# Early folds moved to GpSimd, free PSUM banks for the MLP, low value rows copied by DMA: one change to a fused attention, Fourier-mix and MLP kernel

## The chip, the cores and the metric

The kernel runs on one core of one Trainium2 chip. A core has TensorE (PE in the profile; PEld is its weight load), VectorE (DVE), ScalarE (ACT), GpSimd (POOL) and SyncE (SP, which here only issues transfers), and 16 DMA engines that all queues share. The metric is the device time of one execution in microseconds (us), as the median of several runs. For the kernel before, seven runs gave 291.88 to 294.54 us, with a median of 293.13 us.

## The reference, cut to what matters

Inputs are q, k, v of shape (4, 8, 768, 64) in float32, eight memory keys and values for each head, and two MLP weights of 512 x 2048 and 2048 x 512. Batch is 4.

```python
# attention, for chunks of 32 queries: 8 memory rows, 16 rows of left and 8 of right context
scores = scale * np.matmul(q_c, k_full.transpose(0, 1, 3, 2))
a = softmax(scores)                       # with 1e-09 added to the sum
out[:, :, c_start:c_end] = np.matmul(a, v_full)

# x: attention output as (4, 768, 512)
mixed = np.real(np.fft.fft(np.fft.fft(x, axis=1), axis=2))
u = x + mixed
un = (u - u.mean(-1)) / sqrt(u.var(-1) + 1e-06)
return u + np.maximum(un @ w_ch1, 0.0) @ w_ch2
```

So three things are computed for each batch, one after the other: chunked attention, the real part of a two-dimensional Fourier transform over rows and columns, and a normalised MLP with a residual.

## The kernel before, in words

**Attention.** The program goes through 16 pairs of heads, four for each batch; pair n is handled by `attention(n)`. q and k of a pair are loaded as bfloat16 from GpSimd's queue (`e_load_qk`, L324) into three rotating buffers each, and are turned by TensorE (`e_turn_q`, `e_turn_k`, L351) and copied out of PSUM (L360, L379). v of a pair is loaded by seven transfers from SP's queue (`e_load_v`, L333, L337, L342) into one of four buffers `va`. The partitions 0 to 31 of each `va` buffer hold no values and must be zero: ScalarE writes them once (`e_low_rows`, L312). GpSimd or VectorE write the ones and the zero edges (`e_edges`, `e_edge_ones`). For each pair there are two groups g, one for each half of the 768 rows: scores (L392), exponential on ScalarE (L400), values (L416), and a normalisation on VectorE (L426, L427) that writes `xsb`, the 768 x 512 rows of a batch, as six tiles of 128 rows.

**Fourier mix.** The transform is done with tables and uses its symmetries: sums and differences of rows and of columns, called folds, halve the work. For the first batch (`first_fourier`) the folds are done for each row half g as soon as its heads are there. `g_zy` (L556) adds or subtracts column halves of pairs 0 and 1, for parity `par` 0 and 1. `g_ff` with last = 0 (L569, L571, L574) folds the third pair in, and with last = 1 (L573, L574) the fourth. `g_hi` (L590) and `g_lo` (L594) split the result into two float16 parts, and TensorE multiplies with the row tables (`g_row` L614 with the mid column from `g_mid`, and `g_rows` L627). The sums in PSUM are taken out by L500 and L505, and the column tables follow (`e_columns`, L638). The later batches use `fourier(b)` (L488 for the rows), in which half of the rows is also sent through HBM to reverse their order.

**MLP.** VectorE adds the residual and takes the statistics (L644, L652, L653), ScalarE centres (L658), and the tile is turned: by TensorE for the first batch (L665, L676), by a DMA transpose from SP's queue for the others (`e_flip`, L670). `mlp(b)` then does, for two halves of 384 rows, 16 groups of the first product (`e_ch1`, L698, four matmuls a group, tile `ph`), a ReLU on ScalarE (L706), and three groups of the second product (`e_ch2`, L713, 16 matmuls a group, tile `pc`), whose result VectorE scales and adds to `xsb` (L720). The weights come by four transfers each from GpSimd's queue (L906 for the first, L910 for the second).

**PSUM banks.** Four banks serve as two pairs, `acc` and `mlp`. `mtag(b, i)` binds group i of the MLP to a pair: every third group to `acc`, the others to `mlp`. The same pairs hold `ps`, `pm`, `tp` and others.

**Order.** The order of the instructions on each engine is written out before the program is built. Each step is a task given to `Plan.add` with an engine, a cost, the tasks that it follows, the buffers that it takes and gives, and a rank. `Plan.order` walks through time with these costs and puts on each engine the task with the lowest rank that could start. SP's tasks stay in order unless they are loose; MLP groups have the highest ranks and fill what is left on TensorE. `Plan.share` models how transfers of several queues share the DMA engines. When TensorE would have nothing to do between the first scores and the first `lo`, the planner puts in a product of zeros (`e_fill`, L771, tile `idle`); these are fixed in the program. At run time each engine works off its own list in that order and waits on semaphores, so a late instruction holds up all that stand behind it on its engine. A change of one cost or rank can thus move instructions anywhere in the program.

In the profile's names, `in_q_dram` is q, `qs` and `ks` the loaded q and k, `trq` and `trk` their transposes in PSUM, `sc` scores, `e` the exponentials, `xa` and `xo` values in PSUM, `zy`, `ff`, `hi`, `lo` and `hl` the folds and their parts, `ps` rows, `up` and `dn` the taken-out rows, `pm` columns, `un` and `unT` the centred tile and its transpose, `w_sb` both MLP weights.

## Time and profile before

| what | value |
|---|---|
| median of 7 runs | 293.13 us (291.88 to 294.54) |
| the profiled execution's own time | 293.6 us |
| its span, first to last instruction | 291.9 us |
| TensorE busy | 274.7 us, 94% of the span |
| VectorE busy | 164.7 us, 56% |
| ScalarE busy | 164.9 us, 57% |
| GpSimd busy | 48.0 us, 16% |
| granted TensorE clock | 1.00 |
| moved by DMA | 38.36 MB, 131 GB/s over the span |

The page gives, for each engine, the time in which it was busy, a row of digits for 40 equal slices of the span (9 is 90% busy or more), the chain of work that ended last, and groups of like instructions. The time line lists instructions with start and length in us; an entry in brackets is how long the engine stood idle before it and what released it. A table by stretches gives the length of the stretch, then the busy time and the count of each engine, the granted clock, the mean share of the DMA engines and the GB/s. The profile is of one execution; times inside it are counted from the start of the span.

### The profile page before, as it was taken

The numbers are of one execution on the slowest core, as the hardware profiler recorded it, in microseconds if no ns is written. First come the engines' busy times: TensorE is split into PE (matmuls) and PEld (weight loads), VectorE is DVE, ScalarE is ACT, GpSimd is POOL, SyncE is SP. The second block draws the span as 40 slices with busy tenths as digits, with TensorE's granted clock in tenths as the row PEclk, the third lists the DMA queues.
The fourth block names the chain that finished last, engine by engine and source line by source line (L and its number), as shares of the span: only waits on it lengthen the run. The fifth ranks groups of instructions, "written<-read, shape, count | busy, mean of one in ns | idle before, by whom it ended". The sixth has DMA issues, their size and how long they took to land.

```text
span 291.9 us, 7349 instructions
## 1 busy us (share of the span) xinstructions
PE 274.7 (94%) x3055; PEld 173.3 (59%) x3055; DVE 164.7 (56%) x354; ACT 164.9 (57%) x294; POOL 48.0 (16%) x96
## 2 busy tenths in 40 slices
PE   1498998999999999999999999999899999999994
PEld 1376797765566767566777656656554644645641
DVE  7868998952249873948885878864912012012011
ACT  6796537687576586878885246432750721712700
POOL 8825641130222010121010021010020000000000
PEclk9999999999999999999999999999999999999999
DMA  6998999997999987698941357954221504004204
GB/s 102 204 186 139 211 209 195 197 198 150 176 222 272 146 228 105 92 155 218 185 80 61 37 130 196 145 145 108 56 54 72 110 0 122 25 36 108 38 36 108
DMA packets 98689, 38.36 MB, mean 131 GB/s; under 512 B 85728, under 2 KB 93920, under 8 KB 98656
## 3 DMA queue, kind: packets, MB, share of 16 engines
q1 hardware_dynamic: 87344, 21.83, 40.2%
q0 software_dynamic: 10592, 15.21, 28.3%
q10 hardware_dynamic: 720, 0.85, 0.9%
q8 instruction: 24, 0.39, 0.6%
q14 instruction: 9, 0.07, 0.1%
HBM read 37.36 MB, written 13.37 MB: 174 GB/s over the span
## 4 chain that ended last, share of the span: by engine, by line
PE 88%; DVE 4%; DMA 3%; ACT 1%; POOL 1%; issue 1%; POOLq 0%; DVEq 0%
PE pc L713 29%; PE ph L698 28%; PE xa L416 8%; PE ps L488 5%; PE sc L392 3%; PE pm L638 3%; DMA ks<-in_k_dram 3%; PE trk L351 2%; PE idle L771 2%; PE ps L627 2%; PE trq L351 2%; DVE st L652 1%; DVE xsb L644 1%; PE xo L416 1%; PE ps L614 1%
## 5 line engine op out<-in xcount | busy, mean ns | idle before, releaser
L706 ACT ACTIVATE hT<-ph 128x384 f16<-128x384 f32 x128 | 60.8, 492 | 52.9 <-PE ph L698 52.0
L698 PE MATMUL ph<-unT,w_sb 128*128 128x384 f16 x512 | 88.9, 326 | 0.9 <-ACT hT L706 0.6
L713 PE MATMUL pc<-w_sb,hT 128*128 128x512 f16 x384 | 88.0, 380 | 0.0
L698 PEld LDWEIGHTS <-w_sb 128*128 128x128 f16 x512 | 48.4, 98 | 33.2 <-issue 1.8
L713 PEld LDWEIGHTS <-hT 128*128 128x128 f16 x384 | 35.9, 98 | 40.6 <-issue 0.4
L720 DVE SCALAR_TENSOR_TENSOR osb<-pc,rstd,xsb 128x512 f32<-128x512 f32 x24 | 18.0, 749 | 72.4 <-PE pc L713 69.7
L400 ACT ACTIVATE e<-sc,mbias 128x384 f32<-128x384 f32 x64 | 33.6, 578 | 12.5 <-PE sc L392 12.0
L416 PE MATMUL xa<-va,e 128*64 128x65 f32 x672 | 26.5, 229 | 1.2 <-issue 1.2
L416 PEld LDWEIGHTS xa<-va,e 128*64 128x64 f32 x672 | 22.5, 141 | 8.2 <-issue 6.6
L658 ACT ACTIVATE un<-xsb,mu_s 128x512 f16<-128x512 f32 x24 | 17.2, 721 | 14.2 <-DVE mu_s L653 14.2
L500 ACT CAST up<-ps 128x386 f16<-128x386 f32 x16 | 9.7, 605 | 16.9 <-PE ps L488 15.6
L652 DVE BATCH_NORM_STATS2 st<-xsb 128x6 f32<-128x512 f32 x24 | 16.6, 690 | 0.7
L324 POOL DMA_DIRECT2D qs<-in_q_dram x16 | 10.5, 658 | 36.6 <-PE trq L351 21.9
L360 ACT COPY qT<-trq 128x768 bf16<-128x768 bf16 x16 | 12.7, 796 | 6.1 <-PE trq L351 6.1
L427 DVE TENSOR_TENSOR xsb<-xa,zs 128x384 f32<-128x384 f32 x28 | 15.6, 557 | 1.0
L505 DVE TENSOR_TENSOR up<-ps,up 128x386 f16<-128x386 f32 x16 | 9.5, 594 | 10.7 <-ACT up L500 10.7
L426 DVE RECIPROCAL zs<-xa 128x6 f32<-128x6 f32 x28 | 5.3, 190 | 17.4 <-PE xa L416 17.0
L351 PE MATMUL trq<-ident_b,qs 96*64 96x96 bf16 x256 | 9.1, 218 | 5.6 <-DMA qs<-in_q_dram 5.6
L324 POOL DMA_DIRECT2D ks<-in_k_dram x16 | 10.2, 638 | 22.6 <-PE trk L351 18.9
L379 ACT COPY kTb<-trk 128x1056 bf16<-128x1056 bf16 x12 | 12.5, 1040 | 2.2 <-PE trk L351 2.2
L644 DVE TENSOR_TENSOR xsb<-pm,xsb 128x512 f32<-128x512 f32 x15 | 10.1, 670 | 5.2 <-PE pm L638 5.2
L478 DVE TENSOR_TENSOR lo<-ff,hi 128x768 f16<-128x768 f32 x12 | 11.4, 954 | 2.5 <-ACT hi L473 2.2
(142 smaller groups left out, 327.3 us busy)
## 6 DMA issues: line engine op xcount, KB each, us to landing
va<-in_v_dram SPq DMA_DIRECT2D x32, 220.0 KB
w_sb<-in_moe_w_ch_dram POOLq DMA_DIRECT2D x8, 512.0 KB, 15.3
qs<-in_q_dram POOLq DMA_DIRECT2D x16, 192.0 KB, 6.2
ks<-in_k_dram POOLq DMA_DIRECT2D x16, 192.0 KB, 6.0
out_dram<-osb SPq DMA_DIRECT2D x12, 256.0 KB
x_rows<-xsb POOLq DMA_DIRECT2D x3, 768.0 KB, 5.1
xr<-x_back POOLq DMA_DIRECT2D x3, 768.0 KB, 5.5
out_rows<-osb SPq DMA_DIRECT2D x9, 256.0 KB
```

The costliest lines, as they stand in the source:

```text
L324: nc.gpsimd.dma_start(dst[n % NS][0:QP], src[b, 2 * pr:2 * pr + 2].rearrange("h (p j) d -> p h (j d)", j=RB))
L351: nc.tensor.transpose(out_[64 * hh:64 * hh + 64, j * w:(j + 1) * w], src[:, hh, j * D:(j + 1) * D], eye)
L400: nc.scalar.activation(e1[:, :, :, ts(half, 32)], sc[:, :, 0:6, ts(half, 32)], AFT.Exp, bias=mbias[:, half:half + 1], scale=1.0 / math.sqr ...
L416: nc.tensor.matmul(xa[64 * half:64 * half + 64, st, hh, 0:65], e1[:, hh, t6, :], v1[:, hh, 6 * g + t6, 0:65], start=True, stop=True)
L427: nc.vector.tensor_tensor(xs[b][:, 3 * g:3 * g + 3, 2 * pr * D:(2 * pr + 2) * D] .rearrange("p s (h d) -> p s h d", h=2), xa[:, :, :, 0:D] ...
L488: nc.tensor.matmul(out_[:, sp, :], part[:, ab, sp * 3 + st, c0:c1], tab[:, sp, st, :], start=(st == 0 and i == 0), stop=(st == 2 and i == 1))
L652: nc.vector.bn_stats(st6, xs[b][:, kt, :])
L658: nc.scalar.activation(un, xs[b][:, kt, :], AFT.Identity, bias=mu_of[b][:, kt, 0:1], scale=-1.0)
L698: nc.tensor.matmul(ph[:, 0:384], w1_sb[:, dt, ts(ht, P)], unT_of[b][:, dt, sh * 384:(sh + 1) * 384], start=(dt == 0), stop=(dt == NDT - 1))
L706: nc.scalar.activation(hT_of[b, sh][:, ht, :], ph[:, 0:384], AFT.Relu, bias=0.0, scale=-1.0)
L713: nc.tensor.matmul(pc_of[b, sh, stl], hT_of[b, sh][:, ht, ts(stl, P)], w2_sb[:, ht, :], start=(ht == 0), stop=(ht == NHT - 1))
L720: nc.vector.scalar_tensor_tensor(osb, pc, rstd_of[b][:, st:st + 1], xs[b][:, st, :], ALU.mult, ALU.add)
```

## The change

Three things are changed in what is computed where, and the planner's model is changed beside them.

1. The early folds of the first batch's second row half (`g_zy` with g = 1, and `g_ff` with g = 1 and last = 0) run on GpSimd and no longer on VectorE. Their tasks get ranks 20.1 to 20.3.
2. An MLP group no longer has a fixed pair of banks. `pick` names both pairs, and `Plan.order` takes the one whose bank has been free longest.
3. The low rows of `va[2]` and `va[3]` are filled by transfers from `va[0]` and `va[1]` on SP's queue, and no longer by ScalarE.

In the planner, the weight with which a transfer shares the DMA engines is now given for each task (`grain`) where it was fixed by queue, some costs of transfers are changed, and a DMA transpose holds SP for its cost. A path in which q and k are turned by DMA transposes is added for batches from `TURNED` = 9 on; there are four batches, so it isn't taken, but its two buffers `kU` are zeroed by GpSimd (`t_uz`).

```diff
     def e_low_rows(i):
         low = va[i][0:MEM0].rearrange("p h t c -> p (h t c)")
+        if i > 1:
+            nc.sync.dma_start(low, va[i - 2][0:MEM0].rearrange("p h t c -> p (h t c)"))
+            return
         nc.scalar.copy(low, zero[0:MEM0].to_broadcast([MEM0, 2 * NT * 66]))
...
-        xb, sl = xs[0], slice(3 * g, 3 * g + 3)
-        nc.vector.tensor_tensor(zy_of[0, par][:, sl], xb[:, sl, 0:P], xb[:, sl, HD:HD + P],
+        xb, sl, eng = xs[0], slice(3 * g, 3 * g + 3), nc.gpsimd if g == 1 else nc.vector
+        eng.tensor_tensor(zy_of[0, par][:, sl], xb[:, sl, 0:P], xb[:, sl, HD:HD + P],
                                 ALU.add if par == 0 else ALU.subtract)
...
+        eng = nc.gpsimd if g == 1 and not last else nc.vector
...
-        nc.vector.tensor_tensor(ff[:, :, 1:P], (ff if last else zy)[:, :, 1:P],
+        eng.tensor_tensor(ff[:, :, 1:P], (ff if last else zy)[:, :, 1:P],
                                 rev_ap(xb, 2 * P - 1 + HD * last, P - 1, [[DM, 3]]),
                                 ALU.add if plus else ALU.subtract)
...
-    def mtag(b, i):
-        return "acc" if i % 3 == 2 else "mlp"
+    pick_of = {}
+
+    def pick(*key):
+        return pick_of.setdefault(key, dict(of=("mlp", "acc")))
...
-        ph_of[b, sh, ht] = ph = bank(mtag(b, ht), [P, 512], FP32, "ph")
+        ph_of[b, sh, ht] = ph = bank(pick(b, sh, ht)["tag"], [P, 512], FP32, "ph")
...
-            pc_of[b, sh, stl] = bank(mtag(b, stl), [P, DM], FP32, "pc")
+            pc_of[b, sh, stl] = bank(pick(b, sh, stl, 0)["tag"], [P, DM], FP32, "pc")
...
-        t_low[i] = add("ACT", 1.45, lambda i=i: e_low_rows(i), [t_zero, e_],
-                       rank=(0, 1, 2, 3)[i])
+        t_low[i] = (add("ACT", 1.45, lambda i=i: e_low_rows(i), [t_zero, e_], rank=i) if i < 2 else
+                    add("SP", 0.5, lambda i=i: e_low_rows(i), [t_low[i - 2], e_], moved=0.7,
+                        grain=0.3, loose=True))
...
+    t_uz = add("POOL", 0.4, lambda: [nc.gpsimd.memset(kU[i], 0.0) for i in range(NKU)], rank=20)
...
-    for i in range(2, NV):
-        t_low[i]["behind"] = t_exp[i - 2, 1]
-        t_low[i]["rank"] = t_exp[i - 2, 1]["rank"] + 0.1
...
-                zy = add("DVE", 0.5, lambda par=par, g=g: g_zy(par, g),
+                early = ("DVE", "POOL")[g]
+                zy = add(early, 0.5 + 0.5 * g, lambda par=par, g=g: g_zy(par, g),
                          [t_norm[0, g], t_norm[1, g], t_sines],
-                         take=("unT",) if g == 0 else ())
+                         take=("unT",) if g == 0 else (), rank=20.1 if g else None)
                 for ab in range(2):
-                    pre[par, ab, g] = add("DVE", 0.62 if ab == 0 else 0.5,
+                    pre[par, ab, g] = add(early, (0.62 if ab == 0 else 0.5) + 0.5 * g,
                                           lambda par=par, ab=ab, g=g: g_ff(par, ab, g, 0),
-                                          [zy, t_norm[2, g]],
+                                          [zy, t_norm[2, g]], rank=20.2 + 0.1 * par if g else None,
```

In the planner, the choice of a bank and the new weight of a transfer read:

```diff
+                    take = t["take"]
+                    if t["pick"] is not None:
+                        take += tuple(sorted((x for x in t["pick"]["of"] if self.free[x] > 0),
+                                             key=lambda x: (since.get(x, []) + [0.0])[0]
+                                             + t["pick"]["of"].index(x) * 0.5))[:1] or ("",)
...
-            heads = [xs_[0] + [2.0 if q == "POOL" else 1.0] for q, xs_ in left.items() if xs_]
+            heads = [xs_[0] + [xs_[0][0]["grain"]] for q, xs_ in left.items() if xs_]
...
-                t_un[kt] = add("SP", 0.1, lambda kt=kt: e_flip(b, kt),
-                               [un, t_un.get(kts[i - 1]) if i else None],
-                               take=("unT",) if i == 0 else (), give=("un",), moved=0.8,
+                t_un[kt] = add("SP", 1.2, lambda kt=kt: e_flip(b, kt),
+                               [un], behind=t_un.get(kts[i - 1]) if i else None,
+                               take=("unT",) if i == 0 else (), give=("un",), late=1.6,
                                loose=True)
```

## The prediction

> **What bounds the kernel now.** I read four views: the page's slices and chain, the engines' busy time by stretches that I chose after reading the chain, the time line around 17 to 47 us, and TensorE's waits.
>
> ```profile
> PE 274.7 (94%) x3055; PEld 173.3 (59%) x3055; DVE 164.7 (56%) x354; ACT 164.9 (57%) x294; POOL 48.0 (16%) x96
> ...
> PE   1498998999999999999999999999899999999994
> ...
> PE 88%; DVE 4%; DMA 3%; ACT 1%; POOL 1%; issue 1%; POOLq 0%; DVEq 0%
> ```
>
> TensorE carries 88% of the chain. So the question is only where TensorE stands still, or runs the zero matmuls of L771 ("idle") that produce nothing. Busy time by stretches (length, TensorE, its weight loads, VectorE, ScalarE, GpSimd, clock, DMA), and then the idle matmuls alone in the same stretches:
>
> ```profile
> 0.00:17.00 17.00, 7.22 (x100) 4.56 (x102) 14.43 (x48) 12.28 (x17) 14.03 (x43) 1.00 0.98 155
> 17.00:34.20 17.20, 15.95 (x370) 12.07 (x369) 13.25 (x33) 12.22 (x20) 6.37 (x14) 1.00 1.03 176
> 34.20:47.30 13.10, 12.25 (x178) 11.10 (x178) 12.53 (x34) 7.95 (x16) 6.37 (x11) 1.00 1.10 206
> 47.30:56.70 9.40, 9.16 (x156) 7.80 (x153) 8.40 (x19) 5.40 (x10) 1.44 (x3) 1.00 1.22 198
> 56.70:201.00 144.30, 144.30 (x1794) 92.18 (x1793) 98.02 (x190) 93.04 (x167) 18.22 (x26) 1.00 0.83 155
> 201.00:210.00 9.00, 8.11 (x59) 5.29 (x57) 6.96 (x16) 4.90 (x11) 0.00 (x0) 1.00 0.29 71
> 210.00:287.70 77.70, 77.69 (x415) 40.33 (x413) 10.36 (x17) 29.16 (x60) 1.60 (x2) 1.00 0.26 64
> ...
> 17.00:34.20 17.20, 4.95 (x24) 1.00 1.03 176
> ```
>
> From 56.7 us (the first MLP matmul) to 287.7 TensorE loses 0.9 us in all. What a reordering can win after 17 us is therefore bounded: 17 to 34.2 us holds 1.25 idle and 4.95 of idle matmuls, 34.2 to 47.3 holds 0.85, 47.3 to 56.7 holds 0.24, 201 to 210 holds 0.89: 8.2 us together. In 34.2 to 47.3 VectorE is busy 12.53 of 13.10 us beside a TensorE that is busy 12.25: two engines close to full.
>
> **The trace around the edited steps** (start, length, engine, line, tiles):
>
> ```profile
> 17.85 1.50 ACT L312 COPY va<-zero 32x1584 f32<-32x1584 f32 x1
> 21.80 1.49 ACT L312 COPY va<-zero 32x1584 f32<-32x1584 f32 x1
> ...
> 31.84 0.55 DVE L574 TENSOR_TENSOR ff<-ff,xsb 128x381 f32<-128x381 f32 x1
> 31.95 0.50 POOL L600 TENSOR_TENSOR mid<-xsb 128x3 f32<-128x3 f32 x1 [1.85 <-DVE xsb L427]
> 32.79 0.20 POOL L603 TENSOR_TENSOR mid<-mid,mid 128x3 f16<-128x3 f32 x1
> ...
> 36.74 1.02 DVE L574 TENSOR_TENSOR ff<-zy,xsb 128x381 f32<-128x381 f32 x2
> 37.68 0.55 DVE L556 TENSOR_TENSOR zy<-xsb 128x384 f32<-128x384 f32 x1
> 38.34 1.01 DVE L574 TENSOR_TENSOR ff<-zy,xsb 128x381 f32<-128x381 f32 x2
> ```
>
> The last three lines are the early folds of the second row half: VectorE starts them at 36.67 and is through at 39.27.
>
> **What the Trainium skill says.** (1) "GPSIMD Engine Reference", section 3.1 Elementwise: a two-input tensor_tensor costs GpSimd about 2.6 cycles per element at 1.2 GHz. For 384 elements I estimate 0.83 us, say 0.9 with its start; no run here shows one yet, and VectorE needs 0.5 to 0.55. (2) "SBUF — State Buffer", section Who interferes with whom: a VectorE instruction with two SBUF inputs and a GpSimd instruction that reads SBUF exclude each other; the later one waits for the whole of the other. The trace agrees on GpSimd's side: three elements took 0.50 us at 31.95, ending as VectorE's fold ended (32.39), and a like operation 0.20 at 32.79 beside none. (3) "DMA: Bandwidth & Descriptors", section Issuing engines are not separate DMA queues: transfers from all engines share 16 DMA engines; the trace's DMA share is 0.98 to 1.22 up to 56.7 us, so what is added there delays something.
>
> **The change, part by part.** The planner writes out another order for every engine, so I compared the two built programs' instruction orders.
>
> *Folds.* VectorE loses the 2.60 us block (36.67 to 39.27) and one zy (0.5): 3.1 us. GpSimd gains six two-input folds, 6 x 0.9 = 5.4 us, three small ops, and two memsets of the otherwise unused kU buffers (128x1024 bf16; the nearest row, 4x1024 bf16, took 1.0 each: 2.0 us). The folds of each parity stand between normalisations of pairs 1 to 3 and VectorE's own folds, nearly all of them with two SBUF inputs. Bounds for what this costs VectorE: 0 if they interleave, 5.4 if each GpSimd fold holds VectorE throughout. I take half, 2.7: VectorE comes out 0.4 us ahead instead of 3.1.
>
> TensorE then takes all first-half rows (48 matmuls), mid rows and second-half rows without the transposes that stood between. The 96 rows and 24 mid-row matmuls cost 4 x 1.0 + 4 x 1.0 + 2 x 1.1 = 10.3 us; starting where they start now (34.2) they can't end before 44.5, and end now at 45.3. So even VectorE's full gain would be worth only 0.8 us here. I put 0.5 for TensorE waiting on the lo folds, then 0.95 (evacuation 0.6 at L500 and subtraction 0.6 at L505, less one transpose) before the columns, against 0.85 and 0.24 now: +0.4.
>
> *Low rows.* Removes the two ScalarE copies (1.5 each) at 17.85 and 21.80. The first holds an exponential up (19.25 rather than about 18.75), but the next thing in line is TensorE's gap of 1.24 us at 21.41 in the middle of a value product, released by nothing shown, with a 16 KB instruction packet moving from 20.1 to 21.3: I take it to recur at the same place in the program and to swallow the half microsecond. Two copies of 203 KB enter SP's queue before the third pair's values, which SP now issues from 12.72: about 1.6 us later. They are next needed at 26.3 and 30.1 (L416), and GpSimd's gate on the fourth pair's values moves from 24.93 to some 26.5, behind its zy folds anyway. Cost 0 while those 3 us of cover last, up to 1 without.
>
> *Third pair's ks.* Its transpose now stands ahead of the second score group, at 16.4, when TensorE is still slow (16 transposes 0.88 at 13.09, 0.35 at 19.26): +0.5. It lands at 16.0 now (issue 8.64 plus 7.4), so the bounds are +0.5 and +1.0. The fourth pair's q and k are issued behind the kU memsets, at 17.2 and not 15.2; they land at about 21.4 and 22.8 to 23.4, inside the same gap: 0 to 0.5. Idle matmuls: 24 become 25 after 17 us, with 7 to 4 near 25 us: +0.2 in count, -0.2 since the gap ends the same wait. Sum of these: +0.2 to +0.5; I take +0.2.
>
> *Queue of GpSimd.* The fifth pair's q and k stand where they stood, but the sixth pair's and the four weight loads w1 (L906) now wait for the last folds, so w1 goes from 27.93 to about 38.5: the mid operations end at 34.86, the last parity's folds take 2.0 and up to 0.7 of waiting, the q and k issues 1.3. Now the last chunk lands at 44.1, 16.2 after the first issue, with four q/k loads ahead of it that land some 1.4 apart; with two ahead I expect 52 to 54. The first MLP matmul, which needs all four, comes at about 55.7: covered by some 2 us. w2 and later q/k move with it and are needed later (72 and 79).
>
> *Banks.* `mtag` bound MLP group i to a bank pair; now the planner picks. The one place where TensorE waits for that is 207.7 to 209.6 (waits 0.31 and 0.58): -0.9.
>
> *Order.* Leaving a run of wide matmuls for scores, values or transposes costs 0.1 us each (four pc matmuls 0.97 before a transpose, 0.86 before another wide run). I count 48 such places against 44: +0.4. In the new order the second batch's first MLP group follows its third column group after 6.3 us, not 14.6; its transposed input takes 12.3 us from the first column matmul now (113.7 to 126), 0.85 less without an osb between, just in time at 129: +0.3.
>
> Sum: +0.4 +0.2 -0.9 +0.4 +0.3 = +0.4 us. On the profiled execution: span 291.9 to 292.3, its time 293.6 to 294.0. It lies 0.5 above the median of the runs (293.13), so the median becomes 293.5.
>
> **Rivals.**
> - *Held* (slower). GpSimd's folds hold VectorE for the full 5.4 us: VectorE is 2.3 us worse off, not 0.4 better, a difference of 2.7, of which TensorE passes on 2.2 once its 0.5 is used: 295.7. It decides once a fold takes over 0.9 us and VectorE's neighbours are the lo folds at L594. For: VectorE 96% busy there. Against: several of its operations there read PSUM (L426, L427, L379).
> - *Weights late* (slower). Each microsecond that w1's last landing exceeds 55.7 stops TensorE's queue for one. At 58 it costs 2.3: 295.8. For: DMA share over 1. Against: no weights compete with the value loads before 38 us any more.
> - *Front wins* (faster). The gap at 21.4 doesn't recur (-1.2), VectorE keeps its 3.1 us so the rows run unbroken (-0.5), and the early transpose is not slow (-0.5): 291.3. For: the ScalarE copies were real waits; against: the limit of 44.5 above.
> - *Banks do nothing*: the 0.9 at 208 returns under another name: 294.4, within the same class.
>
> **From cases to numbers.** No change within 0.5% (1.5 us) is what this kernel's measurements can't tell apart. Forecast with the bank variant: 0.45, its own range 292.1 to 294.9, split 0.04 faster, 0.36 same, 0.05 slower. Held 0.18 (0.14 slower, 0.04 same). Weights late 0.14 (0.12 slower, 0.02 same). Front wins 0.23 (0.20 faster, 0.03 same). Sums: faster 0.24, same 0.45, slower 0.31. The range 290.8 to 296.4 reaches into both sides; the unknown fold price and the landing of w1 set its upper end.
>
> **What would show it.** Right: first L698 matmul at 55 to 57 us; TensorE at 100% from there; no wait at 208; L556 and L574 on GpSimd near 0.9 us each, VectorE's L574 and L594 above 0.55 beside them. Wrong: a TensorE wait on w_sb at the first L698; new waits at L416 on va, at L351 on ks near 16.5, or at L698 on unT near 129; a first L698 before 54.5, which would mean the front wins.

## The result and the profile after

The changed kernel takes 295.65 us in the median (294.98 to 297.11) against 293.13 us (291.88 to 295.45): a ratio of 1.0085, 95% interval [1.0064, 1.0106], so 1.9 to 3.1 us slower. The likeliest case of the prediction, 293.5 and no change that can be told, did not come; the time lies in the predicted range. The profiled execution took 295.08 us (span 293.3) against 293.6 (291.9), only 1.5 us more. The ratios here and below leave out executions more than 1.5% above the fastest of their kernel (one of after_again, four of pick_alone, two of the kernel before); the medians keep them.

From the page of the changed kernel, engines and slices of TensorE, then the shares of the chain that ended last:

```profile
PE 276.0 (94%) x3056; PEld 173.1 (59%) x3056; DVE 164.0 (56%) x345; ACT 163.6 (56%) x292; POOL 58.4 (20%) x107
...
PE   1669999999999999979999999999999999999994
...
PE 79%; DMA 10%; POOL 7%; DVE 1%; issue 1%; ACT 1%; POOLq 0%; ACTq 0%
```

TensorE's share of the chain fell from 88% to 79%. DMA now has 10% and GpSimd 7%: the chain runs through the load of the third pair's ks, GpSimd's folds, the w1 loads and a transposing DMA of the second batch. The 7 in TensorE's row, at about 131 us, is new. Busy time in four of the stretches that the prediction used (length, TensorE, weight loads, VectorE, ScalarE, GpSimd, clock, DMA share, GB/s):

```profile
17.00:34.20 17.20, 15.98 (x362) 12.57 (x363) 12.98 (x32) 9.35 (x17) 8.11 (x13) 1.00 0.94 165
...
47.30:56.70 9.40, 8.97 (x152) 6.89 (x150) 8.90 (x21) 6.61 (x10) 2.13 (x3) 1.00 1.07 204
56.70:201.00 144.30, 142.79 (x1811) 89.98 (x1811) 94.28 (x186) 92.76 (x165) 20.51 (x29) 1.00 0.83 158
201.00:210.00 9.00, 9.00 (x74) 6.75 (x73) 4.04 (x7) 5.27 (x11) 0.00 (x0) 1.00 0.30 80
```

The last two rows answer the prediction at once. The 0.89 us at 208 are gone (9.00 of 9.00), and 1.51 us are lost between 56.7 and 201, where the kernel before lost nothing. The idle time in the first two, 1.22 and 0.43, is much as before (1.25 and 0.24). TensorE's waits (what it waited for: us in total, times, longest; the largest, 5.5 us for q at the start, was 5.6 before):

```profile
PE trk L375 <- DMA ks<-in_k_dram: 4.4, 3, 2.7
PE ph L741 <- DMA unT<-un: 1.5, 1, 1.5
...
PE ph L741 <- DMA w_sb<-in_moe_w_ch_dram: 0.4, 1, 0.4
```

TensorE's time line at these places (start, length, engine, line, tiles; in brackets the idle time before and what ended it), first at the third pair's ks, then at the first MLP group, then at the first one of the second batch:

```profile
17.82 0.88 PE L375 MATMUL trk<-turn_b,ks 100*64 100x100 bf16 x16 [2.66 <-DMA ks<-in_k_dram]
...
19.06 1.57 PE L456 MATMUL xa<-va,e 128*64 128x65 f32 x24
...
55.51 0.66 PE L741 MATMUL ph<-unT,w_sb 128*128 128x384 f16 x3
56.60 0.34 PE L741 MATMUL ph<-unT,w_sb 128*128 128x384 f16 x1 [0.43 <-DMA w_sb<-in_moe_w_ch_dram]
...
131.67 0.81 PE L741 MATMUL ph<-unT,w_sb 128*128 128x384 f16 x4 [1.51 <-DMA unT<-un]
```

The first ph starts at 55.51 (55.7 predicted, 56.69 before) and stops within its four matmuls for the last w1 chunk. And GpSimd's time line with the folds and the loads behind them:

```profile
27.05 2.13 POOL L596 TENSOR_TENSOR zy<-xsb 128x384 f32<-128x384 f32 x2 [8.87 <-DVE xsb L467]
...
31.38 1.31 POOL L615 TENSOR_TENSOR ff<-zy,xsb 128x381 f32<-128x381 f32 x1
...
36.20 0.40 POOL L644 TENSOR_TENSOR mid<-mid,mid 128x3 f16<-128x3 f32 x1
...
37.01 2.57 POOL L615 TENSOR_TENSOR ff<-zy,xsb 128x381 f32<-128x381 f32 x2
...
40.83 2.19 POOL L957 DMA_DIRECT2D w_sb<-in_moe_w_ch_dram  x4
```

The six folds (one of 1.28 at 32.69 isn't shown) take 7.3 us, not 5.4; w1 is issued from 40.83, not 38.5. The mid operations, which stand behind four of the folds in this queue, end at 36.60, where they ended at 34.86 before.

**Where the profiled time went.** TensorE's last matmul ends at 289.50 instead of 287.72, 1.8 later, and what follows is 0.4 shorter (3.8 against 4.2).

| term | from | us |
|---|---|---|
| front | first ph 1.18 earlier, but 24 value (0.85), 12 score (0.28) and 16 transposing matmuls (0.46) that stood ahead of it now stand behind | +0.4 |
| wait on w_sb | waits | +0.4 |
| wait on unT | waits | +1.5 |
| bank waits at 208 | stretches | -0.9 |
| more changes of tile shape on TensorE | 102 against 96 after 56.6 us, by 0.1 | +0.6 |
| sum, to compare with 1.8 | | +2.0 |

### The profile page after: what moved, and what is told of

Its sections match the earlier page's. It is cut to its first block, busy times and chain, and to the rows that moved or that the text cites. A ratio compares the mean times of both kernels' runs of the same rounds, so it can differ in the third digit from the quotient of the medians.

```text
span 293.3 us, 7347 instructions
## 1 busy us (share of the span) xinstructions
PE 276.0 (94%) x3056; PEld 173.1 (59%) x3056; DVE 164.0 (56%) x345; ACT 163.6 (56%) x292; POOL 58.4 (20%) x107
## 4 chain that ended last, share of the span: by engine, by line
PE 79%; DMA 10%; POOL 7%; DVE 1%; issue 1%; ACT 1%; POOLq 0%; ACTq 0%
PE ph L741 29%; PE pc L756 27%; PE xa L456 7%; PE ps L528 5%; DMA w_sb<-in_moe_w_ch_dram 5%; DMA ks<-in_k_dram 3%; PE pm L679 3%; PE sc L433 2%; PE trq L375 2%; PE trk L375 2%; DMA unT<-un 2%; POOL ff L615 1%; POOL qs L348 1%; PE pm L579 1%; POOL ks L348 1%
## 5 line engine op out<-in xcount | busy, mean ns | idle before, releaser
L749 ACT ACTIVATE hT<-ph 128x384 f16<-128x384 f32 x128 | 62.3, 491 | 56.0 <-PE ph L741 55.0
L741 PE MATMUL ph<-unT,w_sb 128*128 128x384 f16 x512 | 90.7, 327 | 1.9 <-DMA unT<-un 1.5
L741 PEld LDWEIGHTS <-w_sb 128*128 128x128 f16 x512 | 47.4, 98 | 33.6 <-issue 2.5
L699 ACT ACTIVATE un<-xsb,mu_s 128x512 f16<-128x512 f32 x24 | 17.2, 720 | 6.1 <-DVE mu_s L694 6.1
L375 PE MATMUL trk<-turn_b,ks 100*64 100x100 bf16 x256 | 9.7, 224 | 4.9 <-DMA ks<-in_k_dram 4.4
L348 POOL DMA_DIRECT2D ks<-in_k_dram x16 | 10.3, 642 | 17.0 <-PE trk L375 13.9
```

Of the source, the lines that this page charges most:

```text
L348: nc.gpsimd.dma_start(dst[n % NS][0:QP], src[b, 2 * pr:2 * pr + 2].rearrange("h (p j) d -> p h (j d)", j=RB))
L375: nc.tensor.transpose(out_[64 * hh:64 * hh + 64, j * w:(j + 1) * w], src[:, hh, j * D:(j + 1) * D], eye)
L699: nc.scalar.activation(un, xs[b][:, kt, :], AFT.Identity, bias=mu_of[b][:, kt, 0:1], scale=-1.0)
L741: nc.tensor.matmul(ph[:, 0:384], w1_sb[:, dt, ts(ht, P)], unT_of[b][:, dt, sh * 384:(sh + 1) * 384], start=(dt == 0), stop=(dt == NDT - 1))
L749: nc.scalar.activation(hT_of[b, sh][:, ht, :], ph[:, 0:384], AFT.Relu, bias=0.0, scale=-1.0)
```

## The experiments

Each run edits the changed kernel, unless it says otherwise, and leaves its planner alone: the order is the changed kernel's with the named tasks moved in the list that the planner returns (`behind(t, other)` puts t right after other in that list, which orders each engine's queue). Lines below the edit shift by a few. Ratios are to the kernel before, measured beside each run; "difference" is that ratio times 293.13.

| run | median | ratio, 95% | difference, us |
|---|---|---|---|
| the changed kernel | 295.65 | 1.0085 [1.0064, 1.0106] | +1.9 to +3.1 |
| after_again | 295.80 | 1.0078 [1.0046, 1.0110] | +1.3 to +3.2 |
| k15_late | 294.48 | 1.0049 [1.0027, 1.0071] | +0.8 to +2.1 |
| w1_late | 299.30 | 1.0203 [1.0144, 1.0263] | +4.2 to +7.7 |
| trk_back | 296.41 | 1.0112 [1.0079, 1.0145] | +2.3 to +4.3 |
| clear_trk | 297.10 | 1.0131 [1.0091, 1.0170] | +2.7 to +5.0 |
| no_clear | 296.24 | 1.0115 [1.0081, 1.0148] | +2.4 to +4.3 |
| folds_vector | 296.01 | 1.0114 [1.0079, 1.0150] | +2.3 to +4.4 |
| clear_trk_folds | 297.40 | 1.0150 [1.0121, 1.0179] | +3.5 to +5.2 |
| low_scalar | 294.18 | 1.0046 [1.0031, 1.0061] | +0.9 to +1.8 |
| pick_alone (on the kernel before) | 294.27 | 1.0012 [0.9986, 1.0038] | -0.4 to +1.1 |
| three_moves | 293.29 | 0.9997 [0.9974, 1.0020] | -0.8 to +0.6 |
| moves_split | 293.16 | 1.0006 [0.9988, 1.0024] | -0.4 to +0.7 |

**The granted clock.** The table by stretches also shows the clock that TensorE was granted. In some executions it stood at one half for 3.4 us, as here in trk_back:

```profile
25.20:28.60 3.40, 3.40 (x52) 2.22 (x44) 2.42 (x4) 1.05 (x2) 0.71 (x1) 0.50 0.62 131
```

One such stretch brings the mean over an execution to 0.994 or less, and that mean is on record for each execution. Of the 136 executions of the kernel before that were measured beside these runs and enter the ratios, 20 were that low; their median is 294.66 us, against 292.79 for the other 116. The share differs between runs: 11 of 13 executions of trk_back, 5 of 6 of clear_trk, all 5 of clear_trk_folds and 4 of 6 of w1_late were that low, against 5 of 12 of the changed kernel, 8 of 22 of k15_late and 4 of 22 of low_scalar. So the medians of those four runs hold more than the wait that was moved; whether their order brings the stretches on isn't shown. In the changed kernel itself the low executions are no longer than the others (295.60 and 295.82).

**after_again**: no edit.

> The changed kernel once more, unedited, as the base for the other runs. Its profiled execution was only 1.5 us above the one of before, while the medians stand 2.5 us apart. If the three waits that I blame (third pair's ks 2.7 us, w_sb 0.4, unT 1.5) belong to the order of the instructions, they come back within 0.5 us each, at 295.0 to 296.3. If they are chance, at least one of them moves by more than 1 us, and the difference of the medians is no sum of fixed waits.

Its waits of TensorE, in the view of waits:

```profile
PE ph L741 <- DMA unT<-un: 1.4, 1, 1.4
PE ph L741 <- DMA w_sb<-in_moe_w_ch_dram: 1.1, 1, 1.1
...
PE ps L655 <- POOL mid L643: 0.5, 1, 0.5
```

The unT wait is fixed (1.4), the third pair's ks is waited for 1.6 us after 2.7, which is just over the bound set for chance, w_sb grows from 0.4 to 1.1, and a wait is new: the first row matmuls stop 0.7 us for the mid operations (0.5 for the one shown, 0.2 for the next), which stand behind two folds on GpSimd. This execution took 296.1 us. So part of the 1.0 by which the medians differ more than the first profiled executions did is that the first execution of the changed kernel caught its waits short. How much lies on the other side is shown further down.

**k15_late**: the last pair's ks is loaded later.

```diff
+        behind(T["k", 15], t_rstd[1])
```

> The change with one load moved: the last pair's ks (192 KB) is issued behind the second batch's rstd on GpSimd, at about 130.6 instead of 125.65; it is used at about 165. If the fourth transposing DMA of the second batch lands late (4.9 us after its issue, 2.9 before the change) because that load runs beside it, the wait of the first ph of the second batch falls from 1.5 to 0.3 or less and the time by 1.0 to 1.5 us. If the transposing DMA is slow by itself or behind the next one in its own queue, the wait stays within 0.3 of 1.5 and the time within 0.4.

The first ph of the second batch in TensorE's time line:

```profile
128.32 2.76 PE L756 MATMUL pc<-w_sb,hT 128*128 128x512 f16 x12
131.10 0.81 PE L741 MATMUL ph<-unT,w_sb 128*128 128x384 f16 x4
```

No wait stands ahead of it any more. The fourth transposing DMA was issued at 127.59 and the ph ran on at 131.10, so it landed within 3.5 us; in the changed kernel it was issued at 126.66 and released TensorE only at 131.6, 4.9 later. One 192 KB load issued a microsecond ahead of it made the difference: three_moves and moves_split, which hold the same edit, have no such wait either, and the nine traces of the changed kernel's order with that load ahead stop there for 1.0 to 1.6 us. TensorE ends 0.6 to 1.6 us earlier than in the two executions of the changed kernel, the ratio is lower by 0.3%, about 0.9 us, with intervals that just overlap.

**w1_late**: the w1 wait doubled.

```diff
+        for i in (0, 1):
+            todo.pop(at((T["q", 6], T["k", 6])[i]))
+            todo.insert(at(t_w1[0]), (T["q", 6], T["k", 6])[i])
```

> The change with the seventh pair's q and k issued ahead of the four w1 chunks instead of behind them: w1 starts 1.4 us later, with 384 KB more ahead of it (some 2 us), so it should land 1.4 to 3 us later than 56.55. If w1 is on the path, as the 0.4 us wait says, TensorE's wait on w_sb grows by the same 1.4 to 3 us, and the time grows by as much, to 297.1 to 298.7. If TensorE's loss there is taken up by waits later on (unT at 131.7 has 1.5 us to give), the time grows by 0 to 1.5 us less than the wait.

The first ph group in TensorE's time line:

```profile
59.03 0.34 PE L741 MATMUL ph<-unT,w_sb 128*128 128x384 f16 x1 [1.79 <-DMA w_sb<-in_moe_w_ch_dram]
```

The last chunk was issued at 44.75 and landed 14.2 later; in the changed kernel 42.44 and 14.1, in after_again 42.87 and 14.8. Its landing follows GpSimd's queue one to one, and TensorE is behind it. The unT wait did not shrink (1.6), so nothing takes the loss up later. The median of 299.3 is above the range expected, but the two executions without a stretch at half the clock took 297.58 (the profiled one) and 298.35, inside it; the four with a mean clock of 0.983 to 0.987 took 298.66 to 301.12. So the excess goes with the clock. Why this order meets it more often isn't settled.

**trk_back**: the early transpose of the third pair's ks undone.

```diff
+        behind(T["trk", 2], T["trq", 2])
+        behind(T["kT", 2], T["trk", 2])
```

> The change with one thing undone: the transpose of the third pair's ks (16 matmuls) stands behind that pair's q transpose again, as before the change, and the kTb copy on VectorE with it; nothing else moves. TensorE no longer stands at it for 2.7 us. Theory A (the weights and the unT wait set the end, the front is slack behind them): TensorE is 1 to 2 us earlier at 35 us, meets w_sb at the first ph with a wait of 1 to 2 us instead of 0.4, and the time is within 0.5 us of the change. Theory B (the front sets it): the first ph comes 1 to 1.5 us earlier than 55.5, and the time falls by 1 to 1.5 us. Theory C (VectorE, not TensorE, sets the row block at 34.7): the first ps stays at 34.7 and nothing changes, with more idle matmul time in its place.

TensorE's time line behind the transposes:

```profile
23.41 0.53 PE L375 MATMUL trq<-ident_b,qs 96*64 96x96 bf16 x16 [2.36 <-DMA qs<-in_q_dram]
...
25.34 1.57 PE L456 MATMUL xo<-va,e 128*64 128x65 f32 x24
```

No theory foresaw this. TensorE did run ahead, by 2.5 us at 20 us, and then stopped 2.36 us for the fourth pair's qs. The wait had only moved. The first ps came at 36.37, later than the 34.70 and 34.28 of the two executions of the changed kernel, since after that stop TensorE ran at half the clock for 3.4 us (24 value matmuls 1.57 instead of 0.92). In this execution none of the three came: the first ph is at 57.34, and the longer wait on w_sb of theory A is missing (0.4). The times don't decide between A and B: the median is 0.8 above the change, but the two of the 13 executions without the half clock took 294.69 and 295.15, some 0.9 below the seven such executions of the change (295.82). Two are too few to call it a gain.

**clear_trk**: the same, and the two clearings of kU left out.

```diff
+        behind(T["trk", 2], T["trq", 2])
+        behind(T["kT", 2], T["trk", 2])
-    t_uz = add("POOL", 0.4, lambda: [nc.gpsimd.memset(kU[i], 0.0) for i in range(NKU)], rank=20)
+    t_uz = add("POOL", 0.4, lambda: None, rank=20)
```

> The change with the ks transpose of the third pair put back behind its q transpose, and without the two clearings of kU (two buffers that no later step reads; left out here). With the transpose alone put back, TensorE ran on to the fourth pair's q transpose and waited 2.4 us there for qs, issued behind the clearings. If those clearings are what is late next, the fourth pair's q and k are issued 1.8 us earlier, the waits at 21 to 24.5 fall from 3.0 to 1 or less, and the first ps comes at 33 to 34.3 (36.4 with the transpose alone, 34.3 to 34.7 in the change). What becomes of that gain: theory A (w1 sets the first ph) says the first ph still ends at 56.5 to 57.7 with a w_sb wait longer by what the front gained, time within 0.5 of the change; theory B says the time falls by 1 us or more.

TensorE's time line at the same place:

```profile
22.25 0.34 PE L456 MATMUL xa<-va,e 128*64 128x65 f32 x5 [1.25 <-issue]
23.02 0.53 PE L375 MATMUL trq<-ident_b,qs 96*64 96x96 bf16 x16 [0.43 <-DMA qs<-in_q_dram]
```

The waits on the fourth pair fell to 0.9 (0.43 and 0.47), as expected, and the stop of the kernel before came back in their place: in the middle of the value group, after 19 of its 24 matmuls, released by nothing that the profile names. The first ps is at 34.37, no better than in the changed kernel. The first ph is at 55.18, with 0.6 on w_sb. The profiled execution, 294.92, is the fastest of this kernel and the only one of the six without a stretch at half the clock; the others spread to 298.37.

**no_clear**: the clearings left out alone (the last pair of lines above).

> The change without the two clearings of kU alone (two buffers that no later step reads; left out here), everything else as it is. My sum costed them at 0 to 0.5 us: the fourth pair's q and k are issued 1.8 us earlier, and the wait on its ks at 24 (0.4 us in one execution, none in another) goes. Expected: within 0.5 us of the change, 295.2 to 296.2. If the clearings are what costs the front its time, the first ps comes 1 us or more earlier than 34.3 and the time falls by 0.8 to 1.5 us.

The first ps came at 34.99, in an execution that stood at half the clock from 19.6 to 23.0 and stopped for 0.5 us as described below. The interval overlaps the changed kernel's: no worth of the clearings can be measured in the changed order, which agrees with the 0 to 0.5 us of the sum.

**folds_vector**: the six early folds on VectorE again.

```diff
-        xb, sl, eng = xs[0], slice(3 * g, 3 * g + 3), nc.gpsimd if g == 1 else nc.vector
+        xb, sl, eng = xs[0], slice(3 * g, 3 * g + 3), nc.vector
...
-        eng = nc.gpsimd if g == 1 and not last else nc.vector
+        eng = nc.vector
...
+        for par in range(2):
+            for x in (("zy", par, 1), ("pre", par, 0, 1), ("pre", par, 1, 1)):
+                todo.pop(at(T[x]))
+                todo.insert(at(T["ff", 0, 0, 1]), T[x])
```

> The change with the six early folds of the second row half on VectorE again, as one block ahead of the late folds, where the kernel before had four of the six; GpSimd's queue is 6.5 us shorter, so w1 is issued some 5 us earlier. Theory Weights (w1's landing behind the first ph's other inputs costs 0.4 to 1.1 us and varies from run to run): w1 lands near 51 to 53, no wait on w_sb, the time falls by 0.8 to 1.2 us from the change, and the rows, with VectorE 3 us fuller, give back at most 0.8. Theory Held (GpSimd's folds hold VectorE as long as they save it): the late folds return from 1.0 to 0.5 us each and VectorE's busy time in 34.2 to 47.3 stays within 0.5 us of 12.4, the rows are not later at all, and the time falls by the whole 1.1 or more. If the folds on GpSimd did help TensorE, the first pm comes 1 us or more later than 46.5, and the time is the same or above.

The late folds L615 in VectorE's time line, here (three):

```profile
39.73 1.48 DVE L615 TENSOR_TENSOR ff<-ff,xsb 128x381 f32<-128x381 f32 x3
```

and in the changed kernel, beside GpSimd's folds at 37.01:

```profile
37.39 3.07 DVE L615 TENSOR_TENSOR ff<-ff,xsb 128x381 f32<-128x381 f32 x3
```

Two of the three took 1.34 us instead of 0.54 while GpSimd's folds ran; with a copy of 0.98 instead of 0.22 at 27.29 VectorE was held for 2.4 us. With w1 issued from 36.1, 4.7 earlier, no wait on w_sb is left. Yet the time is not lower (1.0114 against 1.0078 and 1.0085, intervals overlapping), for VectorE and ScalarE now hold TensorE up in the rows and ahead of the columns, 1.4 us in three waits, of which the longest is:

```profile
PE ps L668 <- DVE lo L635: 0.6, 1, 0.6
```

So in these executions the folds on GpSimd gave TensorE about what they cost at w1 (0.4 to 1.1). This answers to none of the three theories alone.

**clear_trk_folds**: the edits of clear_trk and folds_vector together.

> The two edits before together: ks transpose back, no clearings of kU (left out, nothing reads them), and the six folds on VectorE with w1 some 5 us earlier. If the front and w1 are two lanes that meet at the first ph, this run gains what neither does alone: first ph at 54 to 55 without a w_sb wait, and the time 1.5 to 2.5 us below the change. If VectorE sets the rows once the front is earlier, the first ph stays at 55.5 or later, and the time is that of the folds on VectorE alone, within 0.5 us.

TensorE's time line:

```profile
23.64 0.34 PE L456 MATMUL xa<-va,e 128*64 128x65 f32 x5 [2.96 <-issue]
```

Neither outcome: the first ph came at 58.31. The stop sits at the same matmul and lasts 2.96 us, and from 24.1 to 27.5 TensorE stood at half the clock. Against clear_trk (first ps at 34.37, first ph at 55.18) the first ps is 1.6 later, at 35.94; the other 1.6 us up to the first ph go with the waits of folds_vector in the rows and ahead of the columns, which are back (0.6, 0.4 and 0.4). So the front met a third limit, named next, before the two lanes could meet.

**The stop between instructions.** The trace lists, among the DMA packets, some of 16,384 bytes that carry instructions. In all five runs in which TensorE stopped for nothing named, it stopped at the same place of its program, ahead of the 20th matmul of the second pair's first value group, and went on 1.3 to 1.5 us after such a packet was through:

| run | packet moved | TensorE went on | later by |
|---|---|---|---|
| before | 20.10 to 21.27 | 22.65 | 1.38 |
| clear_trk | 19.48 to 20.82 | 22.25 | 1.43 |
| clear_trk_folds | 21.05 to 22.26 | 23.64 | 1.38 |
| no_clear | 21.23 to 22.81 | 24.15 | 1.34 |
| moves_split | 21.74 to 22.78 | 24.23 | 1.45 |

The Trainium skill, "Runtime: NRT & Kernel Launch", section Terms, says that each engine's instructions lie in a memory that is refilled in blocks of 16 KiB; the packets agree in size. The trace does not say whose instructions a packet carries; the 24 of this size in each trace are, by my estimate, 64 bytes for each of TensorE's 6112 matmuls and weight loads. In none of the 14 traces did TensorE reach that matmul less than 1.34 us after the packet. So I take it that a TensorE that comes there ahead of the packet waits, and that a gain made earlier is lost there. No run moved the packet by itself. In the changed kernel it came late because of ks (22.70 for the whole group, packet 20.60 to 21.70) and did not stop. pick_alone has the very instructions of the kernel before in this stretch; its packet moved at 18.12 to 19.11, there was no stop, and its first ps came at 31.74 instead of 33.90. Of these 2.2 us, 0.7 stood already at the start of the group, from a shorter wait ahead of the second pair's ks transpose; 1.5 go with the stop. So the front of one and the same program varies by 2 us from one execution to another, and the profiled execution of the kernel before is one with a late packet. That may be the other side of the difference between medians and profiled executions; one further execution doesn't show it.

**low_scalar**: the low rows by ScalarE, in its idle time.

```diff
-        if i > 1:
-            nc.sync.dma_start(low, va[i - 2][0:MEM0].rearrange("p h t c -> p (h t c)"))
-            return
...
+        for i in (3, 2):
+            behind(t_low[i], T["qT", 1])
```

> The change with the low rows of the third and fourth value buffers zeroed by two ScalarE copies (1.5 us each), put where ScalarE stands idle in the changed kernel (15.0 to 19.2), instead of two 198 KB transfers in SP's queue. If those transfers are why the third pair's ks lands at 17.5 to 17.8 instead of 16, TensorE's wait for it falls from 1.6 to 2.7 to 0.5 or less, the fourth pair's qs then holds it for about 1 us instead, and the first ps comes 0.3 to 1 us earlier; the time is the same within 0.5 us where w1 sets the first ph. If ks lands late for another reason, the wait stays.

TensorE's time line at the third pair's ks:

```profile
16.16 0.88 PE L372 MATMUL trk<-turn_b,ks 100*64 100x100 bf16 x16 [0.43 <-DMA ks<-in_k_dram]
```

The third pair's ks is waited for 0.43 us instead of 1.6 to 2.7: it landed at 16.03, where eight of the nine executions with both 198 KB transfers ahead had it at 17.2 to 17.8. The transfers are not the whole cause: folds_vector, the ninth, has both at the same place and got it at 15.81, and moves_split, with neither ahead, at 17.01. The fourth pair's qs held nothing up. With w1 issued at 41.1 to 42.7 as ever, its last chunk landed 13.7 us after its issue instead of 14.1 and 14.8; the weight load of the first group waited 0.4 for it instead of 0.8 and 1.5, and its matmul hardly at all. The first ph is not earlier (55.73). So what this execution gained by then it gained at w1; how transfers issued 28 us before w1 would reach it isn't shown. The time is below the changed kernel's by 0.3 to 0.4% (about 1.1 us; its interval lies under that of the changed kernel and overlaps that of after_again): the "same" of the expectation was wrong. The transfers that I costed at nothing are one of the two largest items, by the times of 22 executions rather than by a wait that can be pointed at.

**pick_alone**: on the kernel before, the free choice of banks alone (the planner writes its own order from the sixth ph group on).

```diff
-    def mtag(b, i):
-        return "acc" if i % 3 == 2 else "mlp"
+    pick_of = {}
+
+    def pick(*key):
+        return pick_of.setdefault(key, dict(of=("mlp", "acc")))
```

> The kernel before with one part of the change alone: the planner's free choice of the bank for each MLP group. The instructions up to the sixth ph group are those of the kernel before, so the front (first ph at 56.7) stays. My sum put -0.9 on this part (the two bank waits at 208 go) and named a rival by which they return under another name. If the sum is right, no bank wait is left after 200 us and the time is 0.5 to 1.2 us below that of the kernel before, unless the new order brings a wait at the first ph of the second batch: then that wait is seen there and the gain shrinks by it. If the rival is right, waits of 0.5 us or more stand elsewhere after 140 us and the time is the same.

The stretch of the bank waits, in the view by stretches:

```profile
201.00:210.00 9.00, 9.00 (x66) 5.86 (x65) 4.67 (x9) 3.72 (x8) 0.00 (x0) 1.00 0.36 89
```

The bank waits are gone and the time is not lower. Its profiled execution took 296.42 us and stood at half the clock from 68.7 to 75.5 us, so it isn't compared as a whole; up to 125 us it shows one new wait, 2.7 us on a value load at 69.55, and none on unT. Whether that wait is in the other executions isn't shown.

**three_moves**: low rows on ScalarE, the last ks later, and the first half's mid operations ahead of GpSimd's second fold.

```diff
-        if i > 1:
-            nc.sync.dma_start(low, va[i - 2][0:MEM0].rearrange("p h t c -> p (h t c)"))
-            return
...
+        for i in (3, 2):
+            behind(t_low[i], T["qT", 1])
+        behind(T["k", 15], t_rstd[1])
+        todo.pop(at(T["mid"]))
+        todo.insert(at(T["fold"]), T["mid"])
```

> The change with the three waits taken away that the runs so far separate, the six folds staying on GpSimd: the low rows of two value buffers by ScalarE in its idle time, the last pair's ks issued behind rstd, and the first half's mid operations on GpSimd ahead of its second fold (two runs showed the first row matmuls waiting 0.7 us for them). If the waits add up, the time is 1.6 (low rows) + 1.3 (ks) + 0.5 to 0.7 (mid) below the change's 295.7, so 292.1 to 292.5, 0.3 to 0.8 below the kernel before. If they share one limit (w1's landing or VectorE's folds behind the rows), the first ph stays at 55.5 or later with a wait on w_sb, and the time is 293.0 to 294.0.

The time is that of the kernel before (0.9997). The waits on unT, w_sb and mid are all gone; what came up instead is in its view of waits:

```profile
PE sc L430 <- ACT e L437: 1.6, 1, 1.6
```

Together the three moves are worth 0.8 to 0.9%, 2.4 to 2.6 us, and undo what the change cost. They do not reach 292.1 to 292.5, and 293.29 is inside the span of the second theory, but not for its reason: the first ph, at 56.66, waited for nothing.

**moves_split**: the same, with one buffer zeroed by ScalarE and the other by a transfer behind the third pair's values.

```diff
-        if i > 1:
+        if i > 2:
             nc.sync.dma_start(low, va[i - 2][0:MEM0].rearrange("p h t c -> p (h t c)"))
...
+        behind(t_low[2], T["qT", 1])
+        behind(t_low[3], t_lv[2])
+        behind(T["k", 15], t_rstd[1])
+        todo.pop(at(T["mid"]))
+        todo.insert(at(T["fold"]), T["mid"])
```

> The three moves together once more, with the low rows mended: two ScalarE copies in a row held up the second exponential by 1.6 us in the run before, so here ScalarE zeroes one buffer (1.5 us, in its idle time ahead of that exponential) and the other is filled by the 198 KB transfer behind the third pair's values instead of ahead of them. If the exponential was what ate the gain, TensorE's wait on it falls to 0.4 or less, the first ph comes at 55 to 55.8, and the time is 0.5 to 1 us below the three moves, 292.2 to 292.8, under the kernel before. If the front has another floor (w1's landing, TensorE's instruction packets), the time stays at 293.0 to 293.6.

TensorE's time line:

```profile
24.23 0.34 PE L456 MATMUL xa<-va,e 128*64 128x65 f32 x5 [1.31 <-issue]
```

The wait on the exponential is gone, the stop between instructions took its place, first ph 57.27, time unchanged: the floor of the second theory. No version here is measurably faster than the kernel before.

## Why the prediction was right or wrong

The range held, but the sum that led to 293.5 did not: of its terms the second batch's input was mis-sized by 1.2 us, and the low rows and w1, which stood at 0, cost about 1.1 and 0.4 to 1.1. Three of the prediction's own signs of being wrong came, the waits on w_sb, on ks near 16.5 and on unT near 129. That *Held* and *Weights late* name 295.7 and 295.8, and 295.65 was measured, is luck: with the folds back on VectorE nothing was won, w1 cost less than half of its 2.3, and the two largest items are in neither rival. Part by part:

- **Banks, -0.9**: the waits went, in every run of the new choice. As a gain it holds inside the sum only; alone on the kernel before it gives nothing that can be measured. *Banks do nothing*, that it returns under another name, is supported by one wait in one execution and not settled.
- **Second batch's input, +0.3**: the right place, the wrong size, and the largest miss: 1.5. "Just in time at 129" took the length of the old chain, 12.3 us less 0.85, from the first column matmul. That matmul came at 117.64, and the chain took 13.9 to release TensorE at 131.6. What it left out was who shares the DMA engines with the fourth transposing DMA; k15_late shows that it was one load of 192 KB.
- **w1 covered by 2 us**: failed first at the step "the mid operations end at 34.86". That is their end in the kernel before; four folds now stand ahead of them in GpSimd's queue, and they ended at 36.60, 1.7 later. The rest is the price of a fold, 0.9: the folds took 1.0 to 1.3 each, 7.3 in all instead of 5.4, and the last parity's 2.6 instead of 2.0. So w1 started 2.3 us later than forecast, and at 14 to 15 us to landing it came at 56.5 to 57.7, not 52 to 54. *Weights late* is what happened, at 0.4 to 1.1 us; w1_late shows that the end follows it.
- **Low rows, 0**: wrong. The step counted what the two transfers do to SP's own queue (1.6 us on values with 3 us of cover) and not what they do to the ks load on GpSimd's, which landed at 17.3 and 17.7 instead of 16.0. The statement about shared DMA engines stood two paragraphs above and was not applied. low_scalar puts the whole at about 1.1 us; how it comes about is shown only in part, by ks.
- **Early ks transpose, +0.5**: a wait of 1.6 to 2.7 us in its place. The conclusion drawn from that, that putting it back would win the time again, did not come true in the median: the fourth pair's q and the instruction packet bound the same stretch, and most of those executions met the half clock.
- **The gap at 21.4, "I take it to recur at the same place in the program"**: the place was right, the condition was missing. In the 14 traces it comes only where TensorE is there before its packet.
- **Front, +0.4 and +0.2 together**: the sum is right in the profiled execution (+0.4 by the account above), by compensating errors: a later ks and no stop for instructions.
- **VectorE, half held, 2.7**: 2.4 measured; the half was a guess that came out near. *Held* falls as a bound of the end: with the folds back on VectorE nothing was won.
- **Order, +0.4**: 0.6 by the count in the trace. The 0.1 us is lost on coming back to wide matmuls too.
- **Kernel-before profile 0.5 above the median**: used as a constant shift for both kernels. It is 0.6 below for the changed one. The sign of such a shift belongs to an execution, not to a kernel.
- ***Front wins***: did not come; no edit of the front alone lowered the median below the changed kernel's except by taking DMA work away. For trk_back and clear_trk this is not the last word, since all but three of their 19 executions met the half clock.

## What to carry to other kernels

When a change adds a transfer or moves one, list every load that is in flight beside it on whatever queue, and give each the added time. Before counting a wait as won, name what stands a few instructions behind it; here ks, the next pair's q and the program's own instruction packet lay within 2 us of each other, and clearing one or two only uncovered the third. A single execution of the kernel before may lie 2 us off in a stretch: where the forecast is 1 us, read such a stretch in two executions. And where the mean clock of each execution is on record, set it beside the times before an edit is given the credit or the blame for 1 or 2 us.

## What the hardware showed

- TensorE stopped at one fixed place of its program until 1.3 to 1.5 us after a 16 KB instruction packet in five traces; the packet's start varied from 17.0 to 21.7 us over all 14. What sets that moment was not tried.
- TensorE's granted clock was 0.50 for 3.4 us in five traces (from 19.2 in k15_late, 19.6 in no_clear, 20.9 in three_moves, 24.1 in clear_trk_folds, 25.2 in trk_back) and for 6.8 us in pick_alone (from 68.7). 24 value matmuls took 1.57 there instead of 0.92, 16 transposes 0.88 instead of 0.52. In each of the six a stop of 1.5 to 3.0 us ended within 2 us of the stretch's start; stops of 1.24 to 1.31 us (before, clear_trk, moves_split) had none behind them, nor had the 1.8 us at w1 in w1_late. The recorded clock doesn't tell all: behind the stop of 2.7 us in the changed kernel 24 value matmuls took 1.57 as well (at 19.06), at a recorded 1.00. The Trainium skill, "TensorE: Matmul & The Clock Gate", section What's actually happening, gives half the clock until some 3.4 us of work and again after an idle window of that order. The length agrees; the stops here were shorter than that window. What starts a stretch is open.
- Each change of tile shape costs TensorE about 0.1 us, in both directions: a wide matmul is followed after 0.255 us by a value matmul and after 0.163 by its like, a score matmul by a wide one after 0.122 where the scores among themselves mean 0.014. The Trainium skill, "TensorEngine Tiling (Array Packing)", section Key Properties, says that changing the tiling mode drains TensorE, without a price; the trace gives one.
- A two-input fold of 128x381 took GpSimd 1.0 to 1.3 us beside VectorE, over the 0.83 estimated in the prediction.
